# Splitting the first rank product and transposing the first pair from x, in a gate-loop and low-rank-mixer kernel

## The chip, the cores and the metric

The kernel runs on one core of one Trainium2 chip. Its time is the device time of one execution in microseconds (us). The engines are called PE (TensorE), DVE (VectorE), ACT (ScalarE), POOL (GpSimd) and SP (SyncE, which here only issues DMAs).

## The reference

The inputs have 4 batches, 8 heads, 768 tokens and a head size of 48. The first part is a recurrence with a complex gate per token and channel:

```
mag   = sqrt(a_re^2 + a_im^2);  scale = min(mag, 0.999) / (mag + 1e-6)
S     = (a_re + i a_im) * scale * S + k_t v_t^T        # state per batch and head, D x D
y_t   = q_t^T Re(S)
```

The heads of y are joined to x of shape (4, 768, 384). The second part mixes tokens by a rank-32 product and then the channels by two matrices:

```
h   = x^T @ U @ V                       # per batch: U is 768 x 32, V is 32 x 768
u   = x + h^T
out = u + relu(u @ w_ch1) @ w_ch2       # 384 -> 1536 -> 384
```

## The kernel before

**Chunks and pairs.** The 768 tokens of a batch are six chunks of 128, so there are 24 chunks. A chunk's way to its x is: loads of q, k, v; gates (magnitudes, products es ps, tot and ph, for two chunks at a time, called a group); prep (weighing, the QKC products, transposes tr into QK); levels and rest (inner, corners, ks, dk, y); and last ACT copies from y into the chunk's x, a tile called xo (L873). When the last chunk of a batch is built, `mixer(m)` is called for the three pairs of chunks of the batch, m = 0, 1, 2 for the first batch.

**The mixer.** For the first pair of a batch it makes the rank sums x^T U in PSUM, in the transposed form (24 matmul instructions in `rank`, L898), and copies them to r (L901). Then for each pair: `spread` multiplies r^T V (L914, 8 instructions), `mixed` adds that to x (xo at the helper line L333), transposes the sum (uTp, L927) and copies it to uT (L929), for both chunks of the pair. uT is what the products "up" (L939) take with w1, and their rectified result h is taken by "down" (L1085 for the first pair, L1128 after it) with w2. uT and h have one buffer each, so the pairs follow one another.

**PSUM.** Banks are given out in classes of two buffers: T for es ps, tot, ph, tr, mixed and uTp, M for up and down, A and Y for a chunk's own products. The rank sums take a T bank before the change.

**Weights.** w1, U and V, and w2 come as 8-byte numbers in 13 pieces: six of w1, one called UV, six of w2. Each piece is loaded into `stage` (two buffers, given out in the order of the pieces), is put through six DVE operations (L487 to L497), and is completed by an accumulating DMA from POOL (L500). V is copied from UV by SP to four places (L517).

**Fills.** Ahead of everything else POOL fills the fixed tiles: GL, QKC, three T, two AT and two DG (L387 to L408). Then it computes `mid` and `total` from `prefix` (L416 to L435).

**The order.** All other work is put on a list with an estimated cost, a rank and what it needs, and a planner (`Plan.order`) plays it through in time: each engine that is free takes the ready operation of the lowest rank. That gives the order in which each engine gets its instructions, and the order is kept. The ranks of chunk work and weights come from a table, URGENCY, by kind and chunk. Work called "small" has the rank m - 1000, that called "mixing" m + 1000. While no mixing work (up, down) has begun and PE has nothing to do, the planner puts in a pair of spare products of the identity with itself (L1252), whose result nobody reads:

```python
elif e == "PE" and now >= self.idle[0] and free[e] <= now and events and not mixing:
    out.append(-1)
```

Of the kernel before, what the change touches and what calls it, by code (L numbers as in the profile page):

```python
# [17 lines left out]
CH = 128  # L18
# [5 lines left out]
BLK = 32  # L24

URGENCY = {
    "w1": {0: -1281.04, 1: -1220.88, 2: -1207.45, 3: 315.61, 4: 369.7, 5: 444.04, 6: 70.95},
    "w2": {0: -1266.56, 2: -21.8, 4: -981.82, 6: -74.99, 8: 354.48, 10: -1170.63, 12: 259.42},
    "gates": {0: 253.11, 1: -1390.93, 2: -0.7, 4: -1280.16, 6: 565.76, 8: -1068.17, 10: -187.84, 12: -54.04, 14: 550.2,
        16: 60.85, 18: -1317.29, 20: 219.78, 22: -1069.82},  # L30
    "angles": {0: -1303.82, 1: -1298.68, 2: -1227.51, 4: 58.46, 6: 57.41, 8: -1315.3, 10: -1053.02, 12: 620.73,
        14: 187.25, 16: -891.55, 18: 148.92, 20: -161.38, 22: -1298.55},
    "prep": {0: -1294.88, 1: 125.6, 2: -26.13, 3: 96.73, 4: 102.92, 5: 146.86, 6: 553.65, 7: 283.9, 8: 120.02,
        9: -991.17, 10: -32.91, 11: 113.94, 12: -202.96, 13: 14.8, 14: 318.58, 15: 357.43, 16: 269.94, 17: 521.08,
        18: 158.53, 19: -163.04, 20: 127.47, 21: 184.1, 22: 205.57, 23: -1204.94},
    "levels": {0: 201.22, 1: 294.56, 2: -15.94, 3: 207.38, 4: -1236.01, 5: 275.3, 6: 572.46, 7: 14.34, 8: -1057.92,
        9: 306.71, 10: 125.53, 11: 133.52, 12: 287.15, 13: 373.35, 14: 82.96, 15: 592.16, 16: 289.79,
        17: -1204.78, 18: -1075.08, 19: 91.86, 20: 733.17, 21: -1309.23, 22: 119.93, 23: -1230.17},
    "rest": {0: 93.55, 1: 47.27, 2: 273.41, 3: 257.67, 4: -1050.04, 5: -1068.08, 6: -1240.77, 7: -1208.87, 8: -1033.73,
        9: -1290.81, 10: 34.85, 11: -1143.56, 12: -162.29, 13: -197.24, 14: -1046.5, 15: 612.4, 16: 244.97,  # L40
        17: -1261.21, 18: 98.64, 19: -1031.75, 20: -1297.46, 21: 239.78, 22: 384.61, 23: 164.23},
}


# [144 lines left out]
def kernel(  # L189
# [200 lines left out]
    nc.gpsimd.tensor_copy(out=tail, in_=ident[:, 127:128].to_broadcast([128, CH]))  # L390
    AT, DG, VP = [], [], []
    QKC = singles.tile([128, H, 2, DP], FP, name="QKC")
    nc.gpsimd.memset(QKC, 0.0)
    GATE = singles.tile([128, 6, GC * DM], FP, name="gate")
    AREA = {nm: GATE[:, n] for n, nm in enumerate(("x", "y", "n", "z", "ar", "ai"))}
    AREA.update({nm: AREA[nm].rearrange("p (c h d) -> p c h d", h=H, d=D) for nm in ("ar", "ai")})
# [1 line left out]
    TS = []  # L398
    for n in range(3):
        TS.append(singles.tile([DQ, GC, H * NTOT], FP, name="T%d" % n))  # L400
        nc.gpsimd.memset(TS[n], 1.0)
    for n in range(3):
        VP.append(singles.tile([128, H, D], FP, name="VP%d" % n))
    for n in range(2):
        AT.append(singles.tile([128, H, HC], FP, name="AT%d" % n))
        DG.append(singles.tile([128, H, BLK], FP, name="DG%d" % n))
        nc.gpsimd.memset(AT[n], 0.0)
        nc.gpsimd.memset(DG[n], 0.0)  # L408

    def constants():  # L410
        SP(0.4, ("load", 0.1), lambda: nc.sync.dma_start(out=prefix, in_=spans[:, PRE * CH:(PRE + 1) * CH]), writes=[("prefix", 0)])
# [464 lines left out]

    def mixer(m):
        i0 = m * MC  # L880
        b, c0 = where(i0)
# [7 lines left out]

        if c0 == 0:  # L890
            buffer(r, "r", 1, [128, DM])
            ps = out_of("rank", b, [128, DM], [128, 512])

            def rank():
                for k in range(NCH // MC):
                    for n in range(NP):
                        c = n % MC * (NCH // MC) + k
                        nc.tensor.matmul(out=get(*ps)[n * R:(n + 1) * R], lhsT=U[:, c], rhs=get("xo", b * NCH + c), start=(k == 0),  # L898
                                         stop=(k == NCH // MC - 1), tile_position=(0, n * R))
            PE(2.0, R0, rank, [("UV", 0)] + [("xo", b * NCH + c) for c in range(NCH)], [ps], steps=2 * NP * NCH // MC)  # L900
            ACT(c_act(DM), R0, lambda: nc.scalar.copy(out=get(*r), in_=get(*ps)), [ps], [r])  # L901
        uT, h = ("uT", m), ("h", m)
        buffer(uT, "uT", 1, [128, KD, N])
        buffer(h, "h", 1, [128, KF, N])

        def spread():
# [12 lines left out]
        def mixed(cc, ps):  # L919
            i, c = i0 + cc, c0 + cc  # L920
            u = ("xo", i)
            DVE(c_dve(DM), R0, lambda: add(get(*u), get(*ps), get(*u)), [ps], [u])
            tr = out_of("uTp", i, [128, KD, CH], [128, 4, CH])

            def turn():
                for f in range(KD):
                    nc.tensor.transpose(out=get(*tr)[:, f], in_=get(*u)[:, f * 128:(f + 1) * 128], identity=ident)  # L927
            PE(0.35, R0, turn, [u], [tr], steps=KD)
            DVE(c_dve(DM), R0, lambda: nc.vector.tensor_copy(out=get(*uT)[:, :, cc * CH:(cc + 1) * CH], in_=get(*tr)), [tr],  # L929
                [uT + (cc,)])  # L930
# [283 lines left out]

    for n, nm in enumerate(AREA):
# [92 lines left out]
```

## Time and profile before

| | us |
|---|---|
| median of 3 runs | 697.34 (695.6 to 698.66) |
| profiled execution | 698.57 |
| its span, first to last instruction | 696.8 |
| PE busy | 673.7 |
| DVE busy | 538.9 |
| ACT busy | 416.5 |
| POOL busy | 51.8 |
| of PE: spare products (L1252) | 57.8 |
| first rank product (L898) | at 133.13 |
| first up product (L939) | at 140.81 |

Times inside the kernel count from the first instruction of the profiled execution. Busy time of an engine is the time in which at least one of its instructions runs; consecutive instructions overlap by a little, so the sum of their durations is larger. The granted clock of PE was 0.997 on average.

### The profile page before, as it was taken

The numbers are of one execution on the slowest core, as the hardware profiler recorded it, in microseconds if no ns is written. First come the engines' busy times: TensorE is split into PE (matmuls) and PEld (weight loads), VectorE is DVE, ScalarE is ACT, GpSimd is POOL, SyncE is SP. The second block draws the span as 40 slices with busy tenths as digits, with TensorE's granted clock in tenths as the row PEclk, the third lists the DMA queues.
The fourth block names the chain that finished last, engine by engine and source line by source line (L and its number), as shares of the span: only waits on it lengthen the run. The fifth ranks groups of instructions, "written<-read, shape, count | busy, mean of one in ns | idle before, by whom it ended". The sixth has DMA issues, their size and how long they took to land.

```text
span 696.8 us, 26972 instructions
## 1 busy us (share of the span) xinstructions
PE 673.7 (97%) x12116; PEld 594.2 (85%) x12116; DVE 538.9 (77%) x877; ACT 416.5 (60%) x776; POOL 51.8 (7%) x92
## 2 busy tenths in 40 slices
PE   8988998999999999999999999999998999999998
PEld 8777777786787888888888888889998898999998
DVE  5899999888998887758598668779886884555734
ACT  7879874968886897958796745434524325031230
POOL 5100000012100010001010100000000000000000
PEclk9999999999999999999999999999999999999999
DMA  8884745699514442432243031222111010000000
GB/s 202 190 187 86 172 99 105 171 222 189 110 36 97 87 92 54 94 70 57 51 89 78 3 86 40 45 43 56 37 36 18 14 41 2 18 7 24 7 18 24
DMA packets 165203, 53.24 MB, mean 76 GB/s; under 512 B 154016, under 2 KB 160352, under 8 KB 165088
## 3 DMA queue, kind: packets, MB, share of 16 engines
q1 hardware_dynamic: 161008, 42.26, 28.0%
q0 software_dynamic: 4080, 9.27, 5.9%
q8 instruction: 95, 1.56, 0.9%
q14 instruction: 20, 0.16, 0.1%
HBM read 33.59 MB, written 4.72 MB: 55 GB/s over the span
## 4 chain that ended last, share of the span: by engine, by line
PE 75%; ACT 10%; DVE 9%; issue 3%; DMA 2%; SPq 0%; DVEq 0%; ACTq 0%
PE down L1128 20%; PE few L997 12%; PE up L939 10%; PE tr L705 6%; PE inner L739 5%; ACT gate L327 4%; PE y L864 3%; PE dk L825 3%; DVE QK L330 2%; PE ks ps L810 2%; PE ph L650 2%; PE es ps L583 2%; PE tot L612 2%; PE y L856 2%; PE spare L1252 1%
## 5 line engine op out<-in xcount | busy, mean ns | idle before, releaser
L330 DVE TENSOR_TENSOR QK<-QK,T 112x1024 f32<-112x1024 f32 x120 | 145.4, 1217 | 7.6 <-PE corners L789 4.0
L939 PE MATMUL up<-uT,w 128*128 128x256 f32 x432 | 98.9, 382 | 0.0
L939 PEld LDWEIGHTS up<-uT,w 128*128 128x128 f32 x432 | 80.5, 190 | 12.3
L1005 ACT COPY h<-few 128x512 f32<-128x512 f32 x36 | 20.6, 586 | 95.0 <-PE few L997 78.2
L708 ACT COPY QK<-tr 112x512 f32<-112x512 f32 x96 | 53.0, 586 | 36.5 <-PE tr L705 36.1
L1128 PE MATMUL down<-w,h 128*128 128x192 f32 x396 | 74.1, 331 | 0.0
L327 ACT ACTIVATE gate<-gate 128x768 f32<-128x768 f32 (+1 forms) x91 | 70.2, 789 | 5.3 <-DMA gate<-in_a_re_dram 2.2
L1128 PEld LDWEIGHTS down<-w,h 128*128 128x128 f32 x396 | 63.7, 190 | 3.2 <-issue 1.1
L739 PEld LDWEIGHTS inner<-QK 112*32 112x32 f32 x4608 | 45.4, 109 | 20.7 <-issue 15.4
L333 DVE TENSOR_TENSOR h<-few,h 128x512 f32<-128x512 f32 x54 | 37.1, 690 | 31.3 <-PE few L997 28.7
L739 PE MATMUL inner<-QK 112*32 112x16 f32 (+1 forms) x4608 | 51.3, 190 | 10.4 <-issue 9.3
L1252 PE MATMUL spare<-ident 128*128 128x128 f32 x406 | 57.8, 289 | 1.7 <-POOL ident masks.py:199 1.5
L330 DVE TENSOR_TENSOR QKC<-qk,cs 128x768 f32<-128x768 f32 x48 | 45.7, 953 | 14.9 <-PE tr L705 13.4
L705 PE MATMUL tr<-ident,QKC 128*112 128x128 f32 x384 | 54.2, 276 | 2.8 <-ACT QK L708 1.1
L1252 PEld LDWEIGHTS spare<-ident 128*128 128x128 f32 x406 | 52.0, 200 | 5.5 <-POOL ident masks.py:199 1.5
L333 DVE TENSOR_TENSOR xo<-down,xo 128x192 f32<-128x192 f32 (+1 forms) x79 | 29.6, 385 | 28.5 <-PE down L1128 28.3
L705 PEld LDWEIGHTS tr<-ident,QKC 128*112 128x112 f32 x384 | 42.1, 133 | 10.9 <-ACT QK L708 3.0
L997 PE MATMUL few<-gate,w 128*128 128x128 f32 x336 | 44.0, 279 | 0.0
L1072 POOL DMA_DIRECT2D out_dram<-xo x32 | 18.8, 586 | 321.0 <-DVE xo L333 289.2
L873 ACT COPY xo<-y 64x192 f32<-64x192 f32 x96 | 30.0, 313 | 18.8 <-PE y L864 17.4
L997 PEld LDWEIGHTS few<-gate,w 128*128 128x128 f32 x336 | 40.6, 194 | 0.5
L1128 PE MATMUL down<-stage 128*128 128x192 f32 x198 | 36.8, 329 | 0.1
(131 smaller groups left out, 1242.6 us busy)
## 6 DMA issues: line engine op xcount, KB each, us to landing
stage<-in_moe_w_ch_dram SPq DMA_DIRECT2D x12, 768.0 KB, 5.8
gate<-in_a_re_dram SPq DMA_DIRECT2D x24, 192.0 KB, 3.5
gate<-in_a_im_dram SPq DMA_DIRECT2D x24, 192.0 KB, 3.7
qk<-in_q_dram SPq DMA_DIRECT2D x24, 192.0 KB, 3.4
qk<-in_k_dram SPq DMA_DIRECT2D x24, 192.0 KB, 4.2
VP<-in_v_dram SPq DMA_DIRECT2D x24, 192.0 KB, 3.4
T<-E SPq DMA_DIRECT2D x48, 96.0 KB, 2.7
w<-stage POOLq DMA_DIRECT2D x12, 384.0 KB, 6.0
```

What stands on the lines that cost most here:

```text
L327: return nc.scalar.activation(out=o, in_=i, func=f, **kw)
L330: nc.vector.tensor_tensor(out=o, in0=a, in1=b, op=OP.mult)
L333: nc.vector.tensor_tensor(out=o, in0=a, in1=b, op=OP.add)
L705: nc.tensor.transpose(out=get(*ps)[0:DQ, j], in_=get(*qkc)[:, hh * HH + j].rearrange("p u d -> p (u d)")[:, 0:DQ], identity=ident)
L708: ACT(c_act(HH * CH) - 0.05, R1, lambda u=u, hh=hh, ps=ps: nc.scalar.copy(out=get(*QK)[:, u, hh * HH:(hh + 1) * HH], in_=get(*ps)[0:DQ]), ...
L739: nc.tensor.matmul(out=get(*ps)[js, h], lhsT=k_of(h)[:, js], rhs=part(q_of(h)[:, js], "p"), start=True, stop=True, tile_position=(0, j * BLK))
L825: nc.tensor.matmul(out=get(*dk[r])[x:end, h], lhsT=get(*ks)[at, h, x:end], rhs=get(*VPi)[at, h], start=True, stop=True, tile_position=(r * ...
L873: ACT(c_act(HH * D), RR, lambda r=r, u=u: nc.scalar.copy(out=get(*xi).rearrange("p (a u d) -> p a u d", u=2, d=D)[r * HC:(r + 1) * HC, :, ...
L939: nc.tensor.matmul(out=get(*ps)[:, e], lhsT=w1[:, f, (ff + e) * 128:(ff + e + 1) * 128], rhs=get(*uT)[:, f], start=(f == 0), stop=(f == KD ...
L997: nc.tensor.matmul(out=get(*ps)[:, q], lhsT=w()[:, q * 128:(q + 1) * 128], rhs=v[0](), start=(n == 0 and q == 0), stop=True, skip_group_ch ...
L1128: nc.tensor.matmul(out=get(*to)[:, part], lhsT=x(j), rhs=y[:, j], start=(first and j == 0), stop=(j == KH - 1), skip_group_check=not first)
L1252: nc.tensor.matmul(out=spare[0], lhsT=ident, rhs=ident, start=True, stop=True)
```

## The change

It has four parts.

1. The rank sums of the first batch are issued in two parts: the first as soon as chunks 0, 1, 3 and 4 are there, the second with chunks 2 and 5. They take an M bank in place of a T bank. The other batches keep one part.
2. `early`, called after chunk 1, transposes x of chunks 0 and 1 and ACT copies the result to uT. When r is there, `ahead` multiplies r^T V in the transposed form, and DVE adds it onto uT. The first pair's `mixed` only adds r^T V to x and returns.
3. The fills of QKC, T, AT and DG are made by DVE in place of POOL.
4. The whole table URGENCY has other numbers, and a new kind, "early".

```diff
@@ URGENCY (all seven kinds have new numbers; a part)
-    "w1": {0: -1281.04, 1: -1220.88, 2: -1207.45, 3: 315.61, 4: 369.7, 5: 444.04, 6: 70.95},
-    "w2": {0: -1266.56, 2: -21.8, 4: -981.82, 6: -74.99, 8: 354.48, 10: -1170.63, 12: 259.42},
-    "gates": {0: 253.11, 1: -1390.93, 2: -0.7, 4: -1280.16, 6: 565.76, 8: -1068.17, 10: -187.84, 12: -54.04, 14: 550.2,
+    "w1": {0: 1414.34, 1: 92.74, 2: 171.13, 3: 523.81, 4: 817.78, 5: 880.63, 6: -1570.73},
+    "w2": {0: 905.49, 2: 125.8, 4: -1333.44, 6: 250.58, 8: -1418.3, 10: -243.54, 12: 248.18},
+    "gates": {0: 389.41, 1: -242.19, 2: -294.92, 4: -1313.92, 6: 1394.01, 8: -136.97, 10: 416.49, 12: 883.07,
...
+    "early": {0: 4.1},
@@ fills
-    nc.gpsimd.memset(QKC, 0.0)
+    nc.vector.memset(QKC, 0.0)
...
-        nc.gpsimd.memset(TS[n], 1.0)
+        nc.vector.memset(TS[n], 1.0)
...
-        nc.gpsimd.memset(AT[n], 0.0)
-        nc.gpsimd.memset(DG[n], 0.0)
+        nc.vector.memset(AT[n], 0.0)
+        nc.vector.memset(DG[n], 0.0)
@@ new functions
+    def early():
+        uT, RE = ("uT", 0), ("early", 0)
+        buffer(uT, "uT", 1, [128, KD, MC * CH])
+        for cc in range(MC):
+            tr = ("uTp", cc)
+            psum(tr, "T", [128, KD, CH], [128, 4, CH])
+
+            def turn(cc=cc, tr=tr):
+                for f in range(KD):
+                    nc.tensor.transpose(out=get(*tr)[:, f], in_=get("xo", cc)[:, f * 128:(f + 1) * 128], identity=ident)
+            PE(0.35, RE, turn, [("xo", cc)], [tr], takes=[uT], steps=KD)
+            ACT(c_act(DM), RE, lambda cc=cc, tr=tr: nc.scalar.copy(out=get(*uT)[:, :, cc * CH:(cc + 1) * CH], in_=get(*tr)), [tr],
+                [uT + (cc,)])
+
+    def ahead():
+        uT, R0, both = ("uT", 0), ("small", 0), [("more", cc) for cc in range(MC)]
+        for ps in both:
+            psum(ps, "T", [128, KD, CH], [128, 4, CH])
+
+        def products():
+            for f in range(KD):
+                for cc, ps in enumerate(both):
+                    at = slice(cc * MC * R, (cc + 1) * MC * R)
+                    nc.tensor.matmul(out=get(*ps)[:, f], lhsT=get("r", 0)[at, f * 128:(f + 1) * 128], rhs=V[at, cc * CH:(cc + 1) * CH],
+                                     start=True, stop=True, tile_position=(cc * MC * R, 0))
+        PE(0.75, R0, products, [("r", 0), ("V", 0)], both, way=5, steps=4 * KD)
+        for cc, ps in enumerate(both):
+            o = lambda cc=cc: get(*uT)[:, :, cc * CH:(cc + 1) * CH]
+            DVE(c_dve(DM), R0, lambda o=o, ps=ps: add(o(), get(*ps), o()), [ps], [uT + (cc,)])
@@ mixer
-            ps = out_of("rank", b, [128, DM], [128, 512])
+            total_ps = "rank", b
+            psum(total_ps, "T" if b else "M", [128, DM], [128, 512])
-            PE(2.0, R0, rank, [("UV", 0)] + [("xo", b * NCH + c) for c in range(NCH)], [ps], steps=2 * NP * NCH // MC)
+            steps = range(NCH // MC)
+            for ks in [steps] if b else [steps[:-1], steps[-1:]]:
+                PE(0.66 * len(ks), R0, lambda ks=ks: rank(ks), [("UV", 0)] + [
+                    ("xo", b * NCH + n * (NCH // MC) + k) for k in ks for n in range(MC)], [total_ps], steps=2 * NP * len(ks))
-        buffer(uT, "uT", 1, [128, KD, N])
+        if m:
+            buffer(uT, "uT", 1, [128, KD, N])
+        else:
+            ahead()
@@ mixed
             DVE(c_dve(DM), R0, lambda: add(get(*u), get(*ps), get(*u)), [ps], [u])
+            if not m:
+                return
@@ chunks
                 if where(i)[1] == NCH - 1:
                     for m in range(i // MC - NCH // MC + 1, i // MC + 1):
                         mixer(m)
+                elif i == MC - 1:
+                    early()
```

More of the change, by code (lines that the diff above doesn't have):

```diff
@@ L26 @@
 URGENCY = {
-    "w1": {0: -1281.04, 1: -1220.88, 2: -1207.45, 3: 315.61, 4: 369.7, 5: 444.04, 6: 70.95},
-    "w2": {0: -1266.56, 2: -21.8, 4: -981.82, 6: -74.99, 8: 354.48, 10: -1170.63, 12: 259.42},
-    "gates": {0: 253.11, 1: -1390.93, 2: -0.7, 4: -1280.16, 6: 565.76, 8: -1068.17, 10: -187.84, 12: -54.04, 14: 550.2,
-        16: 60.85, 18: -1317.29, 20: 219.78, 22: -1069.82},
-    "angles": {0: -1303.82, 1: -1298.68, 2: -1227.51, 4: 58.46, 6: 57.41, 8: -1315.3, 10: -1053.02, 12: 620.73,
-        14: 187.25, 16: -891.55, 18: 148.92, 20: -161.38, 22: -1298.55},
@@ L33 @@
[L33 to L38, printed above, removed]
@@ L39 @@
-    "rest": {0: 93.55, 1: 47.27, 2: 273.41, 3: 257.67, 4: -1050.04, 5: -1068.08, 6: -1240.77, 7: -1208.87, 8: -1033.73,
-        9: -1290.81, 10: 34.85, 11: -1143.56, 12: -162.29, 13: -197.24, 14: -1046.5, 15: 612.4, 16: 244.97,
-        17: -1261.21, 18: 98.64, 19: -1031.75, 20: -1297.46, 21: 239.78, 22: 384.61, 23: 164.23},
+    "w1": {0: 1414.34, 1: 92.74, 2: 171.13, 3: 523.81, 4: 817.78, 5: 880.63, 6: -1570.73},
+    "w2": {0: 905.49, 2: 125.8, 4: -1333.44, 6: 250.58, 8: -1418.3, 10: -243.54, 12: 248.18},
@@ new lines @@
+    "gates": {0: 389.41, 1: -242.19, 2: -294.92, 4: -1313.92, 6: 1394.01, 8: -136.97, 10: 416.49, 12: 883.07,
+        14: 330.59, 16: 76.51, 18: -248.17, 20: 116.71, 22: -94.78},
+    "angles": {0: -1297.29, 1: -92, 2: -366.05, 4: -1574.77, 6: 114.88, 8: -1289.33, 10: -116.44, 12: -49.51, 14: 198.99,
+        16: 214.99, 18: 126.62, 20: -1067.79, 22: -352.56},
+    "prep": {0: -1601.24, 1: 252.4, 2: 727.6, 3: 190.18, 4: 101.08, 5: 601.2, 6: -973.66, 7: -243.15, 8: 212.37,
+        9: -192.92, 10: -229.49, 11: -1587, 12: -87.97, 13: 56.38, 14: 32.64, 15: -372.96, 16: -1052.61,
+        17: 432.66, 18: 90.6, 19: 59.2, 20: 246.52, 21: 111.51, 22: -49.36, 23: -271.38},
@@ new lines @@
+    "levels": {0: 271.91, 1: 389.71, 2: -72.13, 3: -86, 4: -1016.32, 5: -1921.79, 6: -925.24, 7: 180.3, 8: -69.27,
+        9: 910.03, 10: 142.37, 11: -241.29, 12: -192.34, 13: -73.61, 14: 411.3, 15: 246.35, 16: -943.51,
+        17: -1213.68, 18: 169.65, 19: 207.53, 20: 173, 21: -64.59, 22: 404.12, 23: 883.84},
+    "rest": {0: 167.73, 1: 84.71, 2: 284.23, 3: 130.78, 4: -1781.37, 5: -1008.48, 6: -1598.9, 7: 55.18, 8: -357.34,
+        9: -55.19, 10: -140.84, 11: -1374.84, 12: -1841.47, 13: -56.13, 14: -1317.65, 15: 45.4, 16: 447.88,
+        17: -78.55, 18: -1240.77, 19: -1168.69, 20: -1001.28, 21: 789.45, 22: 234.65, 23: 841.92},
@@ L891, in mixer, with rank @@
             buffer(r, "r", 1, [128, DM])
-            ps = out_of("rank", b, [128, DM], [128, 512])
-            def rank():
-                for k in range(NCH // MC):
+            total_ps = "rank", b
+            psum(total_ps, "T" if b else "M", [128, DM], [128, 512])
+            def rank(ks):
+                for k in ks:
                     for n in range(NP):
                         c = n % MC * (NCH // MC) + k
-                        nc.tensor.matmul(out=get(*ps)[n * R:(n + 1) * R], lhsT=U[:, c], rhs=get("xo", b * NCH + c), start=(k == 0),
+                        nc.tensor.matmul(out=get(*total_ps)[n * R:(n + 1) * R], lhsT=U[:, c], rhs=get("xo", b * NCH + c), start=(k == 0),
                                          stop=(k == NCH // MC - 1), tile_position=(0, n * R))
-            PE(2.0, R0, rank, [("UV", 0)] + [("xo", b * NCH + c) for c in range(NCH)], [ps], steps=2 * NP * NCH // MC)
-            ACT(c_act(DM), R0, lambda: nc.scalar.copy(out=get(*r), in_=get(*ps)), [ps], [r])
+            steps = range(NCH // MC)
+            for ks in [steps] if b else [steps[:-1], steps[-1:]]:
+                PE(0.66 * len(ks), R0, lambda ks=ks: rank(ks), [("UV", 0)] + [
+                    ("xo", b * NCH + n * (NCH // MC) + k) for k in ks for n in range(MC)], [total_ps], steps=2 * NP * len(ks))
+            ACT(c_act(DM), R0, lambda: nc.scalar.copy(out=get(*r), in_=get(*total_ps)), [total_ps], [r])
         uT, h = ("uT", m), ("h", m)
-        buffer(uT, "uT", 1, [128, KD, N])
+        if m:
+            buffer(uT, "uT", 1, [128, KD, N])
+        else:
+            ahead()
         buffer(h, "h", 1, [128, KF, N])
```

## The prediction

> **What bounds the kernel now.** I read the page's shares first, then the busy time by stage, and after that the chain of waits around the place that the change touches.
>
> ```profile
> PE 673.7 (97%) x12116; PEld 594.2 (85%) x12116; DVE 538.9 (77%) x877; ACT 416.5 (60%) x776; POOL 51.8 (7%) x92
> ...
> L1252 PE MATMUL spare<-ident 128*128 128x128 f32 x406 | 57.8, 289 | 1.7 <-POOL ident masks.py:199 1.5
> ```
>
> PE looks full, but 57.8 us of it are the spare products of L1252, which compute nothing and are issued only while no mixing work has begun. The stages (columns: PE, PEld, DVE, ACT, POOL busy; clock; DMA share; GB/s):
>
> ```profile
> 0.00:140.80 140.80, 127.71 (x2820) 108.65 (x2821) 124.75 (x191) 109.53 (x204) 17.15 (x40) 1.00 0.70 154
> 140.80:235.00 94.20, 92.79 (x1508) 73.63 (x1507) 82.92 (x119) 72.95 (x126) 10.50 (x13) 1.00 0.57 122
> ```
>
> The cut at 140.8 is the first up product. Up to there PE is busy for 127.71 us, 57.60 of them spare (the same view for L1252 alone), so useful for 70.1 us: **70.7 us are waste**. After it PE has no filler; its idle time in the other 556.0 us is 556.0 - (673.73 - 127.71) = 10.0 us. The time is therefore the fixed PE work plus a waste that lies almost all ahead of the first up product. To gain, that product must come earlier, without PE running dry later and without useful work sliding behind it. VectorE (DVE) is what holds it back: 124.75 of 140.8 us, and full from 40 to 110 us.
>
> The chain just ahead of the first up product (start, length, what):
>
> ```profile
> 131.01 1.07 PE y L864 x32
> 132.08 0.48 PE tot L612 x16
> 132.56 0.64 PE spare L1252 x4
> 133.20 2.37 PE mixed L898 x24
> 135.57 0.86 PE spare L1252 x6
> 136.44 0.90 PE mixed L914 x8
> 137.38 0.41 issue
> 137.79 0.55 DVE xo L333
> 138.34 0.47 DVE stage L491
> 138.81 0.48 DVE uT L929
> 139.42 0.88 PE ph L650 x2
> 140.30 0.67 PE spare L1252 x6
> 140.97 7.77 PE up L939 x36
> ```
>
> The reader is to see one serial stretch: rank sums (L898), r^T V (L914), add to x (xo L333), transposes, copy to uT, up. By the timeline the last x of batch 0 is written at 132.95 us, and up starts at 140.81: 7.86 us.
>
> [...] the first L560 takes 1.76 us beside GpSimd's memsets, the second, of the same shape, 0.35. [...] The trace has only one-column VectorE memsets (0.06 us)[...].
>
> **Part 1, the rank in two parts and the transposes from x.** Step by step against the 7.86 us. The sums of L898 are 24 instructions in 2.44 us; a third stays behind the last x: 0.81. The copy to r took 0.48, with 0.06 and 0.26 us of latency around it: 0.80, unchanged. New: `ahead` multiplies r^T V in the transposed form, six products of 128 columns. L914 issued two instructions per product, 8 of 192 columns, in 0.92 us; 12 of 128 are the same 1,536 columns: 0.92. Two DVE additions onto uT follow, at the 1.02 us of the two xo additions, 0.03 us after the product. With the 0.18 ahead of the chain and the 0.20 before up: 0.18 + 0.81 + 0.80 + 0.92 + 0.03 + 1.02 + 0.20 = 3.96 us. **The first up starts 3.9 us sooner**, at 136.9. An addition can find one unrelated 0.95 us operation ahead of it on DVE, as the uT copies did (0.95 us of L493 between them); either way that is inside 1 us.
>
> What moves: 16 rank products (1.6 us) and six transposes (1.0) go into time that PE now spends on spare products, so they cost nothing; if that cover were gone they would cost 2.6. Two ACT copies of uT (the copy to r, of the same size, took 0.48 us) replace two DVE copies; ACT is busy for 109.53 of 140.8 us, and they are needed only at the end. L914 and the xo additions remain, but behind the first up. So PE's fixed work grows by the 0.92 us of `ahead`. L914 at 0.92 was useful before the cut and is replaced there by `ahead`. The ph product (L650, 0.88 us, at 139.42) hangs on its own ACT chain and falls behind the cut. Waste falls by 3.9 or, if ph slips, by 3.0; less 0.92: net 2.1 to 3.0, and I take **2.5 us**. Waiting on PE: `ahead` takes both T banks of PSUM, which es ps, tot, ph and tr use too; the two spread banks did that already.
>
> **Part 2, the fills.** GpSimd spends 0.95 (QKC) + 2.73 (T) + 1.0 (AT) + 0.6 (DG) = 5.3 us. On VectorE it is 1,024 + 3,072 + 1,024 + 512 = 5,632 elements[...]. VectorE sits idle from 1.0 to 5.21 us[...]. GpSimd's mid and total come some 5 us sooner at most, but es ps (11.8) waits for GL, and tot (16.8) starts 6 us after total is done (10.7). I take **0**[...]. No queue of SP or GpSimd is passed by anything: the T writes by SP come at 18.4 us.
>
> **Part 3, the order.** The diff replaces the whole URGENCY table, so every engine's order may change. Gates of chunk 6 go from 565.76 to 1394.01, w2 0 from -1266.56 to 905.49: they rank behind the work of batch 0. DVE spends ahead of the cut, on what the first up doesn't need, 5.3 us for group 3's gates, 1.9 for weighing chunks 6 and 7, and 7.6 for two pieces of w2 (31.8 us for eight pieces): 14.8 us. ACT's passes for that group (119.71 to 126.46) stand on the chain ahead of x copies. Deferring all this could bring batch 0 forward by 2 to 8 us. But group 3's PE work (es ps 1.8, tot 1.3, ph 0.9: 4.0 us) then slides behind the cut, where it is paid, so a shift of 5 us saves 1. Lower bound -3 (the order loses), upper bound 4; I take **2 us**. Moved DVE work must fit into its 94.20 - 82.92 = 11.3 us of idle time up to 235.
>
> **The sum.** 2.5 + 0 + 2 = 4.5 us. The profiled execution took 698.57 us (span 696.8, 1.77 around it), 1.2 over the median of 697.34. Against it: 694.1; for the median: **692.8 us**.
>
> **Rivals.** (a) **Forecast**, first up near 132 to 137, gain mostly kept: 686 to 693.8, chance 0.55. (b) **Given back.** The first pair's down products (L1085, 158 to 185) follow the staging of w2, whose last accumulating DMA is issued at 172.12 and lands some 6 us later; h has one buffer, so the second pair's up (183.4) can't pass it. The VectorE work up to there is not less than before. An earlier up then only makes PE wait at down, idle where it was spare. For it: DVE at 8 to 10 tenths from 140 to 200, and the w2 ranks, now late. Against: the DVE idle time of 5 us between 140 and 180, and chunk work that PE can take between. Gain 0 to 3 us: 694 to 700, say 696; chance 0.30. (c) **Slower.** The UV piece is the seventh in a ring of two staging buffers, behind w1 pieces 4 and 5, whose ranks go from 369.7 and 444.04 to 817.78 and 880.63. Both the first rank part and `ahead` need it (U, V). Now its last DVE step is at 104.6, its accumulation is issued at 104.95, the V copies at 115.5 to 118.9 and landed by about 122.5: 10.5 us before the last x. If UV slips by more than 10.5 us, each further us delays the first up by one, filled with spare products. A slip of 20 us gives 9.5 - 2.5 = 7 us of loss: 704. Against: UV's own rank falls from 70.95 to -1570.73, and VectorE picks it as soon as it fits. Chance 0.15, with any order that starves PE later. That the early parts land no earlier than before, because the planner puts them just ahead of the last part, is part of (b): the copy of r and the additions would still save about 1 us.
>
> **How the numbers follow.** 0.5%, or 3.5 us, is about what a measurement of this kernel can tell from no change. Faster means below 693.85: 0.55. Within: 0.30. Slower, above 700.8: 0.15. The predicted time is that of (a). The range 686 to 701 leaves out about 0.07 below (parts 2 and 3 both at their better bounds: 2.5 + 1.4 + 4 = 7.9, so 689, with some more for the later stages' 10.0 us of idle) and 0.13 above, in (c).
>
> **What would show it.** Right: 16 L898 products ahead of the last x copy, 8 after; from there to up about 4 us; the first up between 131 and 137; spare under 55 us; idle PE after it still near 10. The first L560 at 0.35 us[...]. Wrong: up earlier but PE idle time growing in the 50 us behind it (b), or the U or V transfer ending the wait for the last rank products (c).

## The result, and the profile after

The changed kernel takes 700.19 us (median of 22 executions, 698.4 to 704.45); the kernel before took 697.31 beside it. The ratio is **1.004, with a 95% interval of 1.0025 to 1.0055**: slower by 0.4%, where 0.65% less was forecast. The profiled execution took 702.3 us, with a span of 700.5.

The shares on the page of the changed kernel (busy us, share, instructions; then the row of the spare products):

```profile
PE 678.3 (97%) x12118; PEld 596.9 (85%) x12118; DVE 542.6 (77%) x885; ACT 417.1 (60%) x778; POOL 46.5 (7%) x84
...
L1300 PE MATMUL spare<-ident 128*128 128x128 f32 x396 | 56.8, 293 | 2.0 <-POOL ident masks.py:199 1.5
```

The busy time by stage, cut at the first up product (columns as before: PE, PEld, DVE, ACT, POOL, clock, DMA share, GB/s):

```profile
0.00:142.20 142.20, 128.10 (x2820) 109.26 (x2820) 125.97 (x195) 106.73 (x202) 12.15 (x32) 0.99 0.67 148
142.20:236.40 94.20, 92.23 (x1461) 71.34 (x1460) 83.08 (x118) 72.72 (x124) 9.55 (x12) 0.98 0.58 123
```

The first up comes at 142.2, 1.4 us later than before and not 3.9 sooner. PE is busy for 128.10 us ahead of it, 56.8 of them spare, so useful for 71.3; the waste is 142.2 - 71.3 = 70.9 us, against 70.7 before. Behind the first up PE is busy for 678.3 - 128.1 = 550.2 us (546.0 before) and idle for 558.3 - 550.2 = 8.1 (10.0 before). Of the 550.2 us, 3.4 are clock that was lost in two stretches at half clock (1.7 in one such stretch before). Two things are new: the clock of 0.99 and 0.98, and the chain ahead of up (start, length, what):

```profile
135.03 0.31 ACT xo L874
135.34 0.02 issue
135.37 0.88 ACT es L328 x2
136.25 0.04 issue
136.29 0.69 PE tot L613 x16
136.98 0.64 PE spare L1300 x4
137.62 0.61 PE tot L613 x16
138.23 0.86 PE spare L1300 x6
139.10 0.87 PE more L909 x12
139.97 1.31 PE spare L1300 x10
141.28 1.00 PE mixed L958 x8
142.28 1.92 PE up L985 x8
```

The last x is written at 135.34, 2.4 us later than before. From there to up it takes 6.9 us, not the forecast 3.96. r is there at 137.0, but `ahead` (more) starts at 139.03: it needs both T banks, and the products tot of chunks 6 and 7 hold them until ACT has read the second at 138.66. With the 0.26 us that the forecast has behind the copy of r, it could have started at 137.26: 1.8 us are lost. A step of a weight piece on VectorE delays the additions onto uT to 140.29: 0.3 us. Then `spread` (mixed L958), which the prediction had put behind the first up, stands ahead of it: the additions end at 141.30, up could start 0.2 us later and starts at 142.2, another 0.7 us. 3.96 + 1.8 + 0.3 + 0.7 = 6.8, and 0.1 is spread over smaller gaps.

Why the last x is late is seen 60 us earlier, in the order of time on PE and on VectorE (start, length, line, operation; in brackets the idle time ahead and what ended it):

```profile
69.91 0.69 PE L740 MATMUL inner<-QK 112*32 112x16 f32 x58 [0.21 <-DVE QK L331]
73.11 0.25 PE L740 MATMUL inner<-QK 112*32 112x16 f32 x6 [2.51 <-issue]
...
73.77 2.90 PE L1300 MATMUL spare<-ident 128*128 128x128 f32 x14
```
```profile
73.40 0.30 DVE L746 COPY_PREDICATED DG<-mask,inner 128x128 f32<-128x128 int32 x1 [2.21 <-PE inner L740]
```

In the middle of 64 short products PE stands for 2.51 us and waits for nothing that the profile shows ("issue"). VectorE, which is busy for 31.16 of the 33.1 us ahead of that (PE for 28.96, spare products included), then stands for 2.21 us. And from 74.09 on PE runs at half its clock, so that 14 spare matmuls take 2.90 us (1.73 in a later run at full clock):

```profile
72.50:75.00 2.50, 1.90 (x18) 1.86 (x18) 1.60 (x3) 2.02 (x6) 0.00 (x0) 0.82 0.86 172
75.00:77.50 2.50, 2.50 (x40) 2.27 (x39) 2.50 (x3) 0.00 (x0) 0.00 (x0) 0.50 0.34 70
```

Such waits come at fixed places. Counted in matmuls from the start, they are ahead of number 349, 1111, 1873, 2127 and 2254 in the changed kernel, 349, 857, 984, 2000, 2127 and 2254 in the kernel before: all multiples of 127 apart. Further on the row shifts by a few matmuls (the waits ahead of 5,045 in the changed kernel and of 10,005 in the kernel before stand 3 and 4 off it). 127 matmuls with their 127 weight loads are 254 instructions. The page lists 95 packets and 1.56 MB on a queue that it names "q8 instruction", 16.4 KB each, and PE's 12,118 matmuls are 95.4 times 127: one packet for each step of the row. At most steps PE doesn't stand for long: the changed kernel has seven waits of 0.55 us or more for nothing that the profile shows, the kernel before nine. This made the theory that the experiments test: **a block of PE's instructions comes late**, where 127 short products are used up quickly (64 of `inner` take 0.7 us) and the transfer of the next block stands behind data.

The dips of the clock lie behind waits. A second wait of this kind, of 1.58 us at 271.55 us, is followed by half clock as well (from 272.06). A third dip, from 179.90, follows a wait of 1.44 us at 179.22, which is for VectorE. Each lasts 3.4 us, which is 1.7 us of clock lost.

### The profile page after: what moved, and what is told of

Read it like the earlier page. It is cut to its first block, busy times and chain, and to the rows that moved or that the text cites. A ratio compares the mean times of both kernels' runs of the same rounds, so it can differ in the third digit from the quotient of the medians.

```text
span 700.5 us, 26991 instructions
## 1 busy us (share of the span) xinstructions
PE 678.3 (97%) x12118; PEld 596.9 (85%) x12118; DVE 542.6 (77%) x885; ACT 417.1 (60%) x778; POOL 46.5 (7%) x84
## 3 DMA queue, kind: packets, MB, share of 16 engines
q8 instruction: 95, 1.56, 0.9%
## 4 chain that ended last, share of the span: by engine, by line
PE 72%; DVE 16%; ACT 8%; issue 4%; DVEq 0%; ACTq 0%
PE down L1174 21%; PE few L1043 12%; PE up L985 11%; PE inner L740 5%; PE tr L706 5%; DVE QK L331 4%; ACT gate L328 3%; PE y L865 2%; PE dk L826 2%; PE ks ps L811 2%; PE spare L1300 2%; PE y L857 2%; PE es ps L584 1%; PE ph L651 1%; PE tot L613 1%
## 5 line engine op out<-in xcount | busy, mean ns | idle before, releaser
L328 ACT ACTIVATE gate<-gate 128x768 f32<-128x768 f32 (+1 forms) x91 | 70.7, 792 | 3.5 <-DMA gate<-in_a_re_dram 1.8
L1300 PE MATMUL spare<-ident 128*128 128x128 f32 x396 | 56.8, 293 | 2.0 <-POOL ident masks.py:199 1.5
L331 DVE TENSOR_TENSOR QKC<-qk,cs 128x768 f32<-128x768 f32 x48 | 45.8, 955 | 10.7 <-PE tr L706 10.2
L328 ACT ACTIVATE h<-h 128x512 f32<-128x512 f32 x36 | 22.6, 631 | 25.8 <-DVE h L334 25.8
```

The lines of the kernel that those rows point to most:

```text
L328: return nc.scalar.activation(out=o, in_=i, func=f, **kw)
L331: nc.vector.tensor_tensor(out=o, in0=a, in1=b, op=OP.mult)
L1300: nc.tensor.matmul(out=spare[0], lhsT=ident, rhs=ident, start=True, stop=True)
```

## The experiments

### One part at a time

The kernel before with the new table and nothing else of the change; with all but the table (rank 4.1 for "early", fills by GpSimd), planned anew; and with VectorE's fills alone.

```diff
order only:  -URGENCY of before            +URGENCY of after, without "early"
parts only:  -URGENCY of after             +URGENCY of before, with "early": {0: 4.1}
             -nc.vector.memset(QKC, 0.0)   +nc.gpsimd.memset(QKC, 0.0)   (T, AT, DG too)
fills only:  -nc.gpsimd.memset(QKC, 0.0)   +nc.vector.memset(QKC, 0.0)   (T, AT, DG too)
```

> The kernel before with nothing changed but the table of ranks (the changed kernel's numbers, without the unused kind early). Theory O (the new order is what loses; the parts gain): 700 to 705 us, 3 us or more over before, since the order carries its late last x and its stalls without the gain of the parts. Rival P (the split, early and ahead lose, the order is neutral or gains): 693 to 697.5.

> The changed kernel with the table of ranks of before (early stays at 4.1) and the fills left on GpSimd: only the split rank, early and ahead. Theory O: 694 to 696 us, the 2 us or so that a shorter way from the last x to up is worth. Rival P: 698 to 701, because ahead waits for both T banks and the first spread still stands ahead of up.

> The kernel before with only the fills of QKC, T, AT and DG moved to VectorE. Both theories: within 1 us of before (696.5 to 698.5); the first es ps starts 0.2 to 0.3 us later (12.07 in place of 11.82). A rival in which the fills set the loss: 699 or more.

| | us | ratio to before |
|---|---|---|
| table only | 708.20 | 1.0154 (1.0130 to 1.0178) |
| parts only, planned anew | 738.52 | 1.0568 (1.0544 to 1.0593) |
| fills only | 698.04 | 1.001 (0.9991 to 1.0028) |

The table alone loses 10.7 us, more than theory O has. The parts with the old table lose 41 us, outside both theories: 17 us of clock in many half clocks, and the first up comes at 151.2, 10.4 us later. Each time the planner also put the other operations into another order, so neither run gives the price of a part; our reading, not tested further, is that a table fits only the list of operations that it was made for. The fills alone can't be told from nothing.

### The chain from the last x to up

The changed kernel, with tot of chunks 6 and 7 moved behind `ahead` and its additions, and the first `spread` behind four up steps. This and the later edits use one function on the finished order; it moves operations, and what depends on them, behind another:

```diff
+    def behind(first, last):
+        moved, at = set(first), final.index(last)
+        keep, late = [], []
+        for n in final[:at + 1]:
+            if n >= 0 and (n in moved or plan.ops[n][5] & moved):
+                moved.add(n)
+                late.append(n)
+            else:
+                keep.append(n)
+        final[:at + 1] = keep + late
+    behind([tot 6, tot 7], second addition of ahead)
+    behind([first spread], up of columns 2 and 3)
```

> The changed kernel with two moves in its finished order: the tot products of chunks 6 and 7 (and what hangs on them) behind ahead and its two additions, so that ahead needs not wait for the banks of tot; and the first spread behind the first two pairs of up columns. If those two waits are the 2.0 and 0.9 us that the first up lost, up starts at about 139.5 in place of 142.2 and the time falls by 1.5 to 2.5 us, to 697.5 to 698.7. If the loss lies only behind the first up: no change, 699.5 to 700.5.

It took 703.55 us (1.0085, 1.0062 to 1.0108), 3.4 us more than the changed kernel, where either less or no change was expected. `ahead` ran at once, 135.81 to 136.75, but three steps of a weight piece stood ahead of the additions on VectorE until 138.44, and the moved tot ahead of up. First up 140.67, 1.5 sooner, with 1.5 us less useful work ahead of it: the waste stayed at 70.9. Behind it PE is idle for 10.3 us in place of 8.1, with new waits of 0.89 us at 147.75 and 0.43 at 151.66. Both waits ahead of up are real, but what was moved away from up is paid behind it, and more.

### Late blocks of instructions

First the blocks were shifted against the work: some of the spare products of the first microseconds were left out (16, 16 and 32 matmuls fewer), which moves every later boundary.

```diff
-    for n in plan.order():
+    final = plan.order()
+    idles = [j for j, n in enumerate(final) if n < 0][::4][:8]     # before 8; after 8 and 16
+    for n in [n for j, n in enumerate(final) if j not in idles]:
```

> The kernel before with every fourth of the first spare products left out, 8 in all (of those that fill PE up to 15 us or so): 32 instructions fewer ahead of everything else on PE, nothing else. If PE's waits for nothing that the profile shows are bound to the place in its instruction stream: the 2.3 us wait at 525.85 and those at 38.56 and 59.66 move or go, and the median moves by 1 to 3 us either way. If they belong to the work at hand: same places, within 0.7 us of before.

> The changed kernel with 8 early spare products (32 PE instructions) left out, its order unchanged. If the waits are bound to the place in the stream: those at 73.1 and 271.5 move or go and the median moves by 1 to 3 us from 700.2. If they belong to the work: unchanged, 699.5 to 700.9.

> The same with 16 early spare products (64 PE instructions) left out. As for 8: another place for the waits and 1 to 3 us either way, or no change.

They took 701.09 (1.0045, 1.0022 to 1.0068), 704.34 (1.0081, 1.005 to 1.0112) and 710.98 us (1.0181, 1.0149 to 1.0212). Nothing but products that nobody reads was taken out. The waits came at counts of the same row, but other ones were long: in the last kernel 3.06 us ahead of matmul 603, within `inner` at 54.03, and 2.02 ahead of 349, where the changed kernel had waited 1.37. They don't tell the boundaries from what else came with fewer early products (half clock from 11.7 us in the first of them and from 13.3 in the third), so the next runs leave PE's count alone.

In the first, one load of a weight piece (768 KB into stage, issued by SP at 63.95 us) goes behind the next two loads, of v and k. In the second, the `inner` of chunks 10 and 11 besides goes behind the products tot that follow it, so that the boundary falls within long work.

```diff
+    behind([load of a weight piece into stage], next load of k)
+    behind([inner of chunks 10 and 11], tot of chunk 15)        # second run only
```

> The changed kernel with one move on SP's queue: the load of a weight piece into stage (issued at 63.95 us, 768 KB) goes behind the two loads of q and k that follow it. PE's instructions and their count stay as they are. Theory A (instruction blocks): PE's wait of 2.51 us at 73.11 us is a block of its own instructions that comes late, because its transfer stands behind this load on the DMA engines. Then the wait shrinks below 1 us, the half clock behind it goes, VectorE does not wait 2.2 us for the inner products, the last x of batch 0 comes near 133.3 in place of 135.34, the first up near 140.2, and the time is 1.5 to 2 us below the changed kernel: 698 to 699. Theory B (order): the wait only fills time that VectorE's order would lose elsewhere; the wait goes and the last x stays within 0.7 us of 135.3, time 699.5 to 701. Theory C: the block is late whatever lies on the DMA engines (short products ahead of it alone): the wait stays above 2 us, time 700.

> As the run with the load moved, and besides the inner products of chunks 10 and 11 (268.77 us in the changed kernel), at whose end the wait of 1.58 us at 271.55 and a half clock of 3.4 us stand, go behind the 32 products tot that follow them. Theory A (instruction blocks): both waits and both half clocks go, which is 1.58 + 1.7 us more than the run with the load moved alone gives: 695 to 696. Theory B (PE has slack there, or the next wait takes its place): no change against that run, 698 to 699. In neither case is the first up moved by the second edit.

They took 698.55 us (1.003, 1.0014 to 1.0046) and **697.88 (1.0021, 1.0006 to 1.0036)**: by the ratios about half of the loss of 0.4% is back (the intervals overlap), without a change to any part of the change. Neither profile has a half clock, and the span of the second is 695.8 us against 700.5. The same place on PE in the second run:

```profile
69.94 0.74 PE L740 MATMUL inner<-QK 112*32 112x16 f32 x64 [0.21 <-DVE QK L331]
...
71.10 1.73 PE L1300 MATMUL spare<-ident 128*128 128x128 f32 x14
```

And the cause, in the DMA view. From 64 to 72 us the changed kernel's DMA engines have busy shares of 1.04, 0.77, 1.05 and 1.10 (stages of 2 us), in the run with two moves 0.71, 0.90, 0.26 and 1.15. The block's packet starts at 70.75 in the changed kernel, when PE has already stood since 70.60, and at 67.92 in the run with two moves; it takes 0.9 us in both. PE began the block before at 65.96 and 65.98. (First line: the half microsecond from 70.5 in the changed kernel; second: from 67.5 in the run with two moves; packets, MB, share.)

```profile
q8 instruction: 1, 0.02, 11.3%
```
```profile
q8 instruction: 1, 0.02, 11.1%
```

With the load out of its way the same block comes 2.8 us sooner, and PE doesn't wait. The packets of this queue, read against the waits in all 20 profiles of this document, say the same: PE has 144 waits of 0.55 us or more for nothing that the profile shows, and 143 of them lie within six matmuls of the row of 127 and end 1.20 to 1.66 us after the end of a packet, one packet further for each boundary (for the 16 in the changed kernel and in the kernel before it is 1.35 to 1.53 us). So what PE waits for there is its block. The last x comes at 133.3 and the first up at 140.15, both 2.1 sooner, and the chain between them is as long as before (6.9). Of the waits and of the first up theory A is right, and theory C falls; with one move the time is inside what it says (698 to 699), with two it came down by less (695 to 696). In the run with one move a new wait for a block, of 1.41 us, came at 78.1 behind a DMA share of 1.16 from 74 to 76, and the last x gained 1.0 in place of 2.1; in the run with two it was 0.80.

The kernel before has such a wait too (2.30 us at 525.85, within `inner`, then half clock, in the profile). There the `inner` went behind two steps of few:

```diff
+    behind([inner of chunks 20 and 21], second few step after it)
```

> The kernel before with one move on PE: the inner products of chunks 20 and 21 (522.32 us, 128 products of 0.01 us), at whose end PE waits 2.30 us for nothing that the profile shows and then runs at half clock, go behind the next two steps of few (16 products of 0.13 us). Theory A: the wait is a block of instructions fetched every 127 products; with 16 long products between, the block is there in time, so 2.30 us and the 1.7 us of half clock are won: 4 us, near 693.3, and no first up moved (140.8). Theory B: VectorE needs these inner products 2 us earlier, so that the delay is paid again at the products that follow, or another wait opens: 696 to 698.

The wait and the half clock are gone from the profile (span 695.3), and the time is 697.19 (1.0008, 0.999 to 1.0026): nothing won. Either most executions of the kernel before lack this wait, or the delayed `inner` costs as much; the run doesn't tell which.

### The parts in the order of before

To price the first part without another table, it was put by hand into the finished order of before: `turn` and its copies behind the last x copies of chunks 0 and 1 (as soon as the T banks are free), two thirds of the rank sums behind those of chunks 0, 1, 3 and 4, `ahead` and its additions where `spread` was, `spread` with `mixed` behind the second up step, and the ph product of chunk 6 behind the first. Table and fills stay.

> The kernel before with its own finished order, into which only the parts are put by hand: the first rank part behind the x of chunk 4, the transposes of chunks 0 and 1 behind the x of chunk 1, ahead and its additions in place of the first spread, and the spread, the xo additions and the ph product of chunk 6 behind the first pair of up columns. No table, no planning anew, fills on GpSimd. If the prediction's step of 3.9 us from the last x to up is right and only the new order lost it: first up at about 136.9, time 694 to 696. If the parts can't gain even so (their banks, the sliding of useful work): 697 to 699.

It took 700.43 us (1.0038, 1.0017 to 1.006), above both expectations. In this run and the next two something else stood in the way. Here, the accumulation of a weight piece (POOL) was issued 1.4 us later than in the kernel before, and a block that had been 0.26 us late there was 2.55 late (first the kernel before, then this run):

```profile
114.91 0.86 POOL L500 DMA_DIRECT2D w<-stage  x1 [9.11 <-DVE stage L497]
```
```profile
122.05 1.05 PE L1252 MATMUL spare<-ident 128*128 128x128 f32 x7 [0.26 <-issue]
```
```profile
116.31 0.85 POOL L501 DMA_DIRECT2D w<-stage  x1 [10.10 <-DVE stage L498]
```
```profile
123.51 1.72 PE L1267 MATMUL spare<-ident 128*128 128x128 f32 x14 [2.55 <-issue]
```

The copy of r, too, had ACT's switch and gate pass ahead of it (PE waited 1.1 us for r). Three runs took these away one by one:

```diff
 second: +behind([switch, gate pass on ACT], copy of r)
         +behind([last VectorE step of weight piece 5], seven operations later)
 third:  +behind([switch, gate pass on ACT], copy of r)
         +behind([GM of chunk 4], last VectorE step of weight piece 5)
 fourth: as the third, and +behind([gate operation L630], additions of ahead)
```

> The kernel before with the two parts of the rank sums and the transposes from x put by hand into its own finished order, and with its own table and fills, as in the held run, but with two things moved: the last VectorE step of weight piece 5, with the accumulation that POOL issues after it (116.31), goes seven VectorE operations later, so that its transfer does not stand ahead of the instruction block that was late at 123.51; and the switch and gate pass on ACT (136.73 to 138.86) go behind the copy of r. Theory A (the parts are worth about the 2.5 us of the forecast once these two are out of the way): the wait at 123.51 shrinks below 1 us, last x near 133.5, up 4 to 5 us after the last x, first up near 138.0 to 138.8, time 694 to 695.5. Theory B (the shorter chain only moves work behind the first up): first up earlier, but time 697 to 698.

> The parts put by hand into the finished order of before, as in the held run (700.4), with the copy of r ahead of the switch and gate pass on ACT, and with the last VectorE step of weight piece 5 one operation earlier in place of seven later: VectorE stands idle there for 1.47 us waiting for the y products, so the step costs nothing, and POOL issues the accumulation near 115 us as in the kernel before, not at 116.31. Theory A (the parts are worth about 2.5 us in an order without a late block there): the wait at 123.5 shrinks below 1.2 us, no half clock before up, first up 138.0 to 139.2, waste near 69, time 694 to 695.5. Theory B (the shorter chain only lets work slide behind up): first up by 139.2 but time 696.5 to 698. Theory C (the late block comes back elsewhere): a wait of over 1.4 us in the 30 us before up, time 698 or more.

> As the third held run (699.8 us), and the VectorE operation of the gates of group 3 (L630, on which the additions onto uT waited for 1.42 us, because ACT's gate pass had gone behind the copy of r) goes behind these additions. Theory A (the parts are worth about 2.5 us once nothing stands in their way in the order of before): first up 4 to 4.5 us after the last x, near 139 to 141 according to how late the last x is; 1.4 us below the third held run and 0.5 us more where no half clock falls into it: 697.5 to 698.5, against 699.8; the waste falls below 72. Theory B (the chain is shorter and work slides behind up): first up earlier by 1.4 us and the time unchanged within 0.7 us of 699.8.

The second took 704.96 us (1.0123, 1.0087 to 1.0158). The weight step, moved later, waited 2.31 us itself and stood ahead of a QK product that the corners wait for; PE stood for 2.30 us at 126.6 with no spare products there, and ran at half clock for 10 us. The third took 699.81 (1.0029, 1.001 to 1.0049): a block came 1.48 us late at 115.25 with a half clock behind it, as theory C has it, and the gate operation L630, for which VectorE now waited on ACT, stood ahead of the additions, and up waited 1.42 us for uT. In the fourth nothing stands between r and up: **697.21 us, ratio 1.000 (0.9984 to 1.0017)**. Its way to up on PE:

```profile
127.66 0.91 PE L584 MATMUL es ps<-GL,mid 128*128 128x384 f32 x2
128.50 1.50 PE L907 MATMUL rank<-xo,UV 128*32 128x384 f32 x16
129.93 1.13 PE L827 MATMUL dk<-VP,ks 64*64 64x48 f32 x32
...
135.25 0.85 PE L907 MATMUL rank<-xo,UV 128*32 128x384 f32 x8
...
136.90 0.94 PE L1320 MATMUL more<-V,r 64*128 64x128 f32 x12
...
139.21 2.76 PE L953 MATMUL up<-uT,w 128*128 128x256 f32 x12
```

From the last x (135.07) to up it takes **4.14 us**, close to the forecast 3.96. But the last x is 2.1 us later than in the kernel before, and the first up gains only 1.6. The second line shows the larger part of the reason: the early part of the rank sums runs for 1.5 us just ahead of chunk 5's dk, whose ks ACT had copied by 128.46. It does not take the place of spare products. (Part of the rest goes with the block at 122 us, 1.11 us late here and 0.26 in the kernel before.) So in a last run it alone went behind chunk 5's y:

```diff
-    put two thirds of rank behind the last of the x copies of chunks 0, 1, 3, 4
+    put two thirds of rank ahead of the first x copy of chunk 5
```

> As the fourth held run (697.2 us, ratio 1.000; last x 135.07, first up 139.21), but the first part of the rank sums (16 products, 1.50 us at 128.50 us) goes from ahead of chunk 5's dk to just behind its last y products, where PE now runs tot and spare products while ACT copies x. Theory A (the first part lay on the way to the last x, so it was not free): dk, y and the last x come 1.2 to 1.5 us sooner, last x near 133.7; the second part then waits for the first, so that the first up gains only 0.6 to 0.9 us: near 138.4, and the time 696.3 to 696.8. Theory B (dk waited for ACT's copy of ks anyway): last x within 0.3 us of 135.07, first up later by up to 0.8 us, time 697.2 to 698.

```profile
128.43 0.91 PE L584 MATMUL es ps<-GL,mid 128*128 128x384 f32 x2
129.28 1.13 PE L827 MATMUL dk<-VP,ks 64*64 64x48 f32 x32
...
136.16 0.85 PE L907 MATMUL rank<-xo,UV 128*32 128x384 f32 x8
```

dk now starts 0.85 us after es ps instead of 2.27, a gain of 1.4, and the last x (134.40) is 0.7 sooner although the block boundary at 123 us fell 0.8 later in this execution. But the second part now waits until 136.16 for the first, tot and four spare matmuls, and the first up comes at 140.11. The last x lies between what theories A and B expect, the first up 0.9 us later than in the fourth run; the time is 697.25 (0.9996, 0.9969 to 1.0024), no difference. Neither place had 1.5 us of PE to give.

### The parts and the fills in the changed order

With both late blocks out of the way, the same two moves were made in the kernel with the new table alone, and in the changed kernel with GpSimd's fills.

```diff
 order and two moves:   table-only kernel   +behind(...) twice, as above
 two moves, POOL fills: run with two moves  -nc.vector.memset(...)  +nc.gpsimd.memset(...)
```

> The kernel before with the changed kernel's table alone (708.2 us, with waits of 2.79 us at 73.14 and 2.49 at 272.95), and in it the same two moves as in the run with two moves: the load of a weight piece behind two loads of q and k, and the inner products of chunks 10 and 11 behind tot. Against that run it lacks the two parts of the rank sums, the transposes from x and VectorE's fills, so the difference of the two is what these bring where the two late blocks are gone. Theory A (parts and fills are worth the forecast 2.5 us, and the rest of the 8 us between 708.2 and 700.2 was late blocks): 700 to 701. Theory B (they are worth nothing, the order is what is left): 697.5 to 698.5. Theory C (they are worth the whole 8 us in this order): 704 to 706.

> The changed kernel with the two moves, and the fills of QKC, T, AT and DG made by GpSimd as before. Theory A (fills bring nothing, as forecast): within 0.7 us of the run with the two moves (697.9); the first es ps near 11.8 in place of 12.1, L561 at 1.76 us the first time. Theory B (fills were what the changed order needs): 1 us slower or more. Theory C (they hold up the start by the time that they take on VectorE): up to 1.5 us faster, first up at or before 139.

They took 703.57 us (1.0079, 1.0051 to 1.0108) and 697.28 (0.9999, 0.9977 to 1.0021). So under the new table the first part is worth 0.8% (5.6 us by the ratios, 6.3 by the medians), between theories A and C and beyond the forecast. The planner made both orders, so this is the part together with what it moved in the plan: last x to up 6.9 us in place of 9.5, the first up at 139.24 in place of 141.25, 1.6 us less idle time and 1.7 less busy time behind it. Without these two late blocks the table alone still costs 5.5 us. VectorE's fills come out at 0.22% by the ratios, 1.5 us, and at 0.6 us by the medians (697.88 with, 697.28 without), from two comparisons whose intervals overlap, so they can't be told from nothing; the first up is at 140.15 with them and 139.24 without.

A last version takes two more waits out behind up, with POOL's fills:

```diff
+    behind([tr of chunk 7], down product that follows)        # PE waited 1.44 us for QKC
+    behind([tot of chunks 10 and 11], down product that follows)
```

> The run with two moves and POOL's fills (697.3 us, ratio 0.9999), with two more moves on PE of the same kind, both behind the first up: the transposes tr at 176.25 us, for which PE waits 1.44 us on VectorE's QKC, go behind the down product that follows them at 177.17, and the products tot at 187.50, into which a block of instructions comes 0.98 us late, go behind the down product that follows them at 189.83. Theory A (PE has no other slack there): 1.44 + 0.98 = 2.4 us less, near 695, and a ratio to before near 0.9965, below 1 with its whole interval. Theory B (the waits move to the next product that needs VectorE): 696.5 to 697.5.

It took 697.04 us (0.9993, 0.9974 to 1.0012). The two waits are gone from its profile, and the time is theory B's. No version beat the kernel before by what can be measured.

## Why the prediction was wrong, step by step

The median of 700.19 us lies inside the range of 686 to 701, near its upper end; that is owed to the width of the range, for the likeliest value, 692.8, and the chances, with 0.55 on faster, had the wrong sign. The sum was 2.5 for the first part, 0 for the fills and 2 for the order. Read as ratios to the kernel before, first part and new table together come to -0.01% (two late blocks out of the way, POOL's fills; -0.23% to +0.21%): neither of the two gains is there. Then come +0.22% for VectorE's fills and +0.19% for the two late blocks, together +0.40%; these two rest on intervals of about 0.2% each side. How the -0.01% is divided depends on the order of the steps. With the table first it is +0.79%, and the first part takes 0.80% back. With the first part first, in the order of before (the fourth held run), it is 0.0%, and the table then adds about nothing (0.9999 against 1.000, each with what stood in its way moved).

- **Part 1, the chain of 3.96 us: right as a sum of operations.** The rank third 1.02 (0.81 forecast), `ahead` 0.94 (0.92), the additions 1.02 (1.02), and 4.14 us for the chain where nothing stands in it. In the changed kernel 2.9 us more stand in it. "`ahead` takes both T banks ...; the two spread banks did that already" is the sentence that failed for 1.8 of them. It compared with the banks that `spread` had taken, and not with who holds the banks at that moment: tot of the next group was issued between. "L914 and the xo additions remain, but behind the first up" failed for another 0.7: `spread` has the rank of "small" work, -1000, and up that of "mixing", so it comes first when r is there.
- **Part 1, "16 rank products ... go into time that PE now spends on spare products, so they cost nothing": wrong by 1.4 us in the order of before.** The prediction named the price if the cover were gone (2.6) but took the spare products of the whole stage as cover. They must be free where the part becomes ready: in the fourth held run the x of chunk 4 comes at 129.1, 6 us ahead of the last x, where PE's order is full.
- **Part 1, net 2.5 us: mis-sized in both directions.** Nothing (-0.2% to +0.2%) in the order of before, though the first up came 1.6 us sooner there, and about 6 us under the new table. In this kernel the part has no price apart from the order that it is put into.
- **Part 2, fills at 0: not contradicted.** Alone they come to 1.001 (0.9991 to 1.0028). The profile of before has no VectorE fill of their size to price them from; measured, they take 5.76 us, from 1.20 to 6.96, where GpSimd's took 5.3. A fill of 1,024 elements takes 0.91 us, with a gap of 0.16 behind it. The 1.4 us that the prediction counts for this part at its best are the 1.76 of the first L560, beside GpSimd's fills, less the 0.35 of the second; with those fills gone the first L561 takes 0.36. The first es ps comes at 12.07 in place of 11.82. The first of the moved fills in the order of time on VectorE, and then the row of L561 (minimum, median and maximum of one in ns):

```profile
1.20 0.91 DVE L394 MEMSET QKC<- 128x1024 f32 x1 [0.18 <-issue]
```
```profile
L561 DVE TENSOR_SCALAR gate<-gate x13: 360/554/562, 7.4 to 388.7; 128x768 f32<-128x768 f32 x11, 128x384 f32<-128x384 f32 x2
```

- **Part 3, the order at -2 us: wrong in its mechanism.** It read two ranks as a deferral of 14.8 us of VectorE work. There was no deferral: ahead of the first up VectorE does five L560 gate operations, eight weighings of q and k and 53 steps of weight pieces in the kernel before, and five, eight and 51 in the changed one; es ps and tot of chunks 6 and 7 still stand ahead of up. The rows of the gate operation up to the first up, before and after (count, busy us, mean ns of one):

```profile
L560 DVE TENSOR_SCALAR gate<-gate 128x768 f32<-128x768 f32 (+1 forms) x5 | 3.8, 752 | 0.0
```
```profile
L561 DVE TENSOR_SCALAR gate<-gate 128x768 f32<-128x768 f32 (+1 forms) x5 | 2.4, 479 | 0.0
```

Measured, the table alone costs 5.5 us without the two late blocks and 10.7 with them; with the first part it comes to nothing. The lower bound of -3 was too narrow: nothing in the profile of before could price a whole new table, so it should have reached as far down as other orders do.
- **Late blocks: no step had them.** The profile of before showed the waits ("0.26 <-issue", "2.30 <-issue"), and its mean clock of 0.997 that some clock was lost, but the working took PE's count of instructions as having no price.
- **The rivals.** (b) didn't happen: idle time behind up fell to 8.1. (c) didn't: V's copies were issued at 117.1 to 119.7, before the first rank part. The slower outcome came by a third way.

## What to carry to other kernels

An operation that is made ready earlier costs nothing only if the engine is free there (1.4 us on PE here, and 1.8 us for two banks, were not): look at the few microseconds where it will be issued, and at who holds its PSUM banks then, not at the idle share of a stage. A rank in a planner's table is not an order: read off where the operations went. A changed order is a change of its own and is compared with the order held fixed, each part put in by hand and each thing that it then collides with named. Where a wait has no releaser, count the engine's instructions up to it; if the counts are a fixed distance apart (127 matmuls here), look for the packets of the instruction queue and at the DMA traffic ahead of each.

## What the runs showed of the hardware that was not expected

- **A block of PE's instructions can come late and stall PE.** In these kernels a boundary every 127 matmuls with their loads costs less than 0.55 us in most places (in all but seven in the changed kernel, all but nine in the kernel before) and up to 3.06 us in some. In these two profiles the five waits of this kind over 1.2 us stand within `inner` (64 products in 0.7 us), and ahead of the longest, 2.51 us, the DMA share was 1.05 and 1.10. PE goes on 1.20 to 1.66 us after the end of the block's packet (143 waits). Moving one 768 KB load by 5.5 us took the wait of 2.51 us away.
- **Some waits of 1.4 us and more have a half clock behind them.** After the wait of 2.51 us at 73.11 the clock was 0.50 for 3.4 us, after 1.44 at 179.22 and 1.58 at 271.55 too. Each of the three took 1.7 us of clock. The length of the wait doesn't decide it: one of 1.73 us at 38.56 in the kernel before left the clock alone, as did others of 1.4 us (38.53 and 177.17 in the run with two moves), one of 2.31 at 72.97 in the run with tot moved and one of 2.79 at 73.14 with the table alone. What decides it was not shown.
- **The same kernel differs by 7 us between executions, in part with its clock.** Of 51 executions of the kernel before (693.4 to 700.8 us), the 22 with a mean clock of 1.0 took 695.0 us in the mean, the four with 0.995 took 698.7. So a single profile can show a half clock that many of the executions don't have.
